# Chunked attention into a token-mixing MLP: k and the two slots of q in three regions, some early clears on ScalarE, a new order of all units

## The chip, the core and the metric

The kernel runs on one core of a Trainium2 chip. The metric is the time of one execution in microseconds of device time. The times before are three runs of the unchanged kernel; the profile is one execution of it.

## The reference

For 8 batches of 8 heads, 576 tokens and a head dimension of 64, attention is computed inside chunks of 64 tokens; its output becomes x, 576 by 512 for each batch. A token mixer then works on x.

```python
scores = scale * np.matmul(q_c, k_c.transpose(0, 1, 2, 4, 3))   # chunks of 64 tokens
attn = np.exp(scores - max); attn = attn / (np.sum(attn, axis=-1, keepdims=True) + 1e-09)
out = np.matmul(attn, v_c)
...
wq = x @ w_q                                  # 512 -> 64
wk = x @ w_k
W_tok = scale * np.einsum('bsd,btd->bst', wq, wk)
mixed = np.einsum('bst,btd->bsd', W_tok, x)
return np.maximum(mixed, 0.0) @ w_out         # 512 -> 512
```

The inputs and the output are float32. The loads cast to float16 on their way.

## The kernel before

**Units.** q and k are cut into 36 units of 1024 rows. A unit is 128 partitions by 512 float16 numbers. All units live in one ring tile, `qk`, with room for 27 units; units 27 to 35 go into the places of units 0 to 8 again. Each unit has three slots: slot 0 holds k, slots 1 and 2 hold q. The rows of q lie in four groups of 32 partitions; groups 0 and 2 go into slot 1, groups 1 and 3 into slot 2, and the other half of each slot must be zero. So there are *clears*: `MZ0_2_1` clears units 0 to 1 of one 32-partition group in the slot that the group's load does not fill (line 145), and `MZ5_9_9` clears both slots of units 5 to 8 at once on 128 partitions (line 142). They are done once; later units land in places whose zeros still stand.

**Loads** (lines 125 to 136) are issued by GpSimd (POOL): `LDk.2_5` brings k of units 2 to 4, `LDq0.2_5` the group 0 of q of the same units, `LDv.12` all of v of batch 1. There are 53 of these loads, the large weight (`LW`) is one more. The loads count on eight semaphores in turn, DMASW0 to DMASW7, so that each issue waits for the landing of the load eight places ahead of it. POOL issues them in order: a load that waits holds up all behind it.

**The chain of one batch.** `TR` (VectorE, DVE, lines 175 and 179) transposes one or two units: first k into a kT tile, then both slots of q into a qT tile. The 20 groups follow the pattern 0-2, 2-4, 4-5, 5-7, 7-9, 9-11, and so on, so that TR0 to TR2 cover units 0 to 4, TR3 and TR4 units 5 to 8, TR5 to TR7 units 9 to 13 (TR7 is unit 13 alone). `SC` (TensorE, PE, line 194) makes the scores of such a group, `EX` (ScalarE, ACT, line 206) the exponentials, `PV` (PE, line 229) the products with v, `RN` (DVE, lines 239 and 240) divides by the sums, three of each for a batch. Then come `XT` (PE transpose), `XE` (its copy), `PJ` and `EP` (projection and copy), `DU`, `WT` and `EW` (a copy and a transpose of the projections), `GM` and `EG` (the product of keys and x), four `MX` with `RL` (mixing and relu) and, 36 in all, `OM` (PE, line 384, the product with w_out) with `OE` (its copy into the ring tile, over units that are no longer needed). `ST` stores three or one of these tiles; all stores wait until the last load of v, `LDv.72`, has landed.

**The order.** Nothing is scheduled by a planner: the string `ORDER` gives the whole program as 430 words, and each engine runs its own words in that order. A letter behind a colon picks the engine of a clear or a copy (D is DVE, A is ACT, P is POOL), a number behind @ picks the PSUM bank. `ZZ4` is four matmuls on a constant tile that nobody reads; they keep TensorE from standing still. `MU` fills that tile, `MO` sets a column of ones in v, `LI` makes identity matrices on POOL, `LS` and `LK` load and cast the small weights. The framework adds semaphore waits between engines: a word that writes a region of a tile waits for the earlier words of `ORDER` that read or wrote it, and one that reads it waits for those that wrote it.

Of the kernel before, what the change touches and what calls it, by code (L numbers as in the profile page):

```python
# [9 lines left out]
F16 = mybir.dt.float16  # L10
F32 = mybir.dt.float32
# [39 lines left out]
def kernel(  # L51
# [10 lines left out]
    nc = tc.nc  # L62
# [3 lines left out]
    P = 128  # L66
# [53 lines left out]
    def load(word):  # L120
# [10 lines left out]
        if it[0] == "k":  # L131
            return nc.gpsimd.dma_start(qk[:, at : at + hi - lo, 0], runs[1][:, lo:hi])
        else:
            i = int(it[1])
            rows = slice(32 * i, 32 * i + 32)
            return nc.gpsimd.dma_start(qk[rows, at : at + hi - lo, 1 + i % 2], runs[0][rows, lo:hi])  # L136
# [388 lines left out]
```

## Time and profile before

| | us |
|---|---|
| median of three runs | 127.6 (126.42 to 129.34) |
| the profiled execution, its own time | 127.21 |
| its span (first to last instruction) | 125.4 |
| PE busy | 95.7 (76%) |
| DVE busy | 92.9 (74%) |
| ACT busy | 67.5 (54%) |
| POOL busy | 49.8 (40%) |

The profiled execution's time is its span and 1.8 us around it. Busy shares are over the whole span; the first matmul starts at 18.05 us and the load queue ends before the stores begin, so the stages have to be looked at one by one. The strips of the profile cut the span into 40 slices of 3.135 us. Sizes of loads in the profile are those in SBUF, in units of 1024 bytes; the rates in its GB/s strip are of bytes written as well.

### The profile page before, as it was taken

To read this page: it belongs to the slowest core of one execution; us is meant where nothing else is said; L and a number is where in the kernel's file an instruction comes from. 1 tells how busy PE (TensorE), PEld (TensorE's weight loads), DVE (VectorE), ACT (ScalarE), POOL (GpSimd) and SP (SyncE) were. 2 spreads that over 40 slices of the span, in tenths; PEclk is the share of its full clock that TensorE was granted. 3 is DMA by queue.
4 is the path that set the end of the run, shared out by engine and by line. 5 is a ranking of instruction groups with operands and counts; after the bars stand their busy time and mean duration, and the time that the engine had idled before them with its cause. 6 is when DMAs were issued, how large, how long until landed. Compare 5 with 4: busy or idle time off the path is not lost.

```text
span 125.4 us, 3815 instructions
## 1 busy us (share of the span) xinstructions
PE 95.7 (76%) x1664; PEld 54.1 (43%) x1664; DVE 92.9 (74%) x136; ACT 67.5 (54%) x111; POOL 49.8 (40%) x64
## 2 busy tenths in 40 slices
PE   0000026788889879988989999999799999999990
PEld 0000024443545555553464555555554756444430
DVE  5402899967687989799899799979698477759220
ACT  0560005212727692498574858989697874544420
POOL 2730799999966139445437684000000000000000
PEclk9999999999999999999999999999999999999999
DMA  2697389999999999999999999999949999119693
GB/s 28 110 186 116 45 67 162 204 180 172 205 202 159 199 200 207 204 184 175 201 188 167 202 205 164 192 182 161 139 83 406 397 417 411 73 63 413 276 368 140
DMA packets 50064, 24.62 MB, mean 196 GB/s; under 512 B 38016, under 2 KB 48256, under 8 KB 50048
## 3 DMA queue, kind: packets, MB, share of 16 engines
q0 software_dynamic: 47456, 14.68, 108.3%
q1 hardware_dynamic: 2592, 9.70, 19.5%
q8 instruction: 13, 0.21, 0.6%
q14 instruction: 3, 0.02, 0.0%
HBM read 29.62 MB, written 9.44 MB: 311 GB/s over the span
## 4 chain that ended last, share of the span: by engine, by line
PE 42%; DMA 19%; POOL 16%; DVE 9%; issue 8%; ACT 4%; DVEq 0%
PE pb L384 21%; DMA wout<-in_moe_w_out_dram 9%; DMA qk<-in_k_dram 7%; POOL qk L136 5%; POOL vt L125 4%; PE pb L250 4%; DMA qk<-in_q_dram 4%; PE pb L276 4%; POOL qk L142 3%; PE pb L348 3%; PE pb L229 3%; PE pb L330 3%; DVE qk L145 2%; PE pb L194 2%; DVE kT L175 2%
## 5 line engine op out<-in xcount | busy, mean ns | idle before, releaser
L384 PE MATMUL pb<-wout,rmx 128*128 128x512 f16 x144 | 35.8, 381 | 0.0
L194 PE MATMUL pb<-qT,kT 64*64 64x128 f16 x576 | 12.9, 229 | 21.1 <-DVE qT L179 20.3
L206 ACT ACTIVATE est<-pb 128x1024 f16<-128x1024 f32 (+1 forms) x20 | 18.5, 941 | 17.7 <-PE pb L194 17.4
L136 POOL DMA_DIRECT2D qk<-in_q_dram x36 | 20.2, 567 | 18.8 <-DMA vt<-in_v_dram 5.9
L240 DVE TENSOR_TENSOR xn<-pb,rec 128x768 f16<-128x768 f32 x24 | 23.0, 957 | 0.8
L175 DVE STREAM_TRANSPOSE kT<-qk 128x512 f32<-128x512 f32 (+1 forms) x20 | 19.9, 997 | 4.4 <-DMA qk<-in_q_dram 3.2
L179 DVE STREAM_TRANSPOSE qT<-qk 128x1024 f32<-128x1024 f32 (+1 forms) x20 | 22.0, 1101 | 0.0
L194 PEld LDWEIGHTS <-kT 64*64 64x64 f16 x576 | 10.4, 113 | 23.5 <-DVE kT L175 17.2
L398 ACT COPY qk<-pb 128x512 f32<-128x512 f32 x26 | 15.1, 591 | 7.8 <-PE pb L384 7.6
L384 PEld LDWEIGHTS <-rmx 128*128 128x128 f16 x144 | 13.2, 104 | 12.3 <-issue 1.2
L125 POOL DMA_DIRECT2D vt<-in_v_dram x8 | 14.7, 1843 | 3.4 <-DMA qk<-in_k_dram 2.4
L266 ACT COPY xT<-pb 128x768 f32<-128x768 f32 (+1 forms) x14 | 9.1, 664 | 11.4 <-PE pb L250 9.6
L364 ACT ACTIVATE rmx<-pb 128x576 f16<-128x576 f32 x20 | 12.6, 653 | 2.7 <-PE pb L348 2.7
L250 PE MATMUL pb<-iden,xn 128*128 128x128 f32 x72 | 11.9, 299 | 0.9 <-DVE xn L240 0.5
L250 PEld LDWEIGHTS pb<-iden,xn 128*128 128x128 f32 x72 | 8.6, 150 | 4.9 <-DVE xn L240 2.4
L396 DVE COPY qk<-pb 128x512 f32<-128x512 f32 x10 | 6.8, 684 | 5.2 <-PE pb L384 5.1
L145 DVE MEMSET qk<- 32x512 f32 (+1 forms) x8 | 4.7, 592 | 7.5 <-DMA qk<-in_q_dram 4.5
L362 DVE TENSOR_SCALAR rmx<-pb 128x576 f16<-128x576 f32 x12 | 8.8, 746 | 1.7 <-PE pb L348 1.6
L417 PE MATMUL pb<-unit 128*128 128x512 f16 x32 | 9.8, 443 | 0.0
L229 PE MATMUL pb<-vt,est 64*64 64x65 f16 x576 | 7.7, 200 | 2.4 <-ACT est L206 2.2
L276 PE MATMUL pb<-xT,wpj 128*128 128x512 f16 (+1 forms) x48 | 9.0, 323 | 0.1
L229 PEld LDWEIGHTS <-est 64*64 64x64 f16 x576 | 6.7, 112 | 5.3 <-issue 3.2
(37 smaller groups left out, 90.7 us busy)
## 6 DMA issues: line engine op xcount, KB each, us to landing
out_dram<-qk SPq DMA_DIRECT2D x11, 768.0 KB, 6.6
vt<-in_v_dram POOLq DMA_DIRECT2D x8, 576.0 KB, 13.2
qk<-in_k_dram POOLq DMA_DIRECT2D x4, 512.0 KB, 12.1
qk<-in_q_dram POOLq DMA_DIRECT2D x16, 128.0 KB, 11.0
qk<-in_k_dram POOLq DMA_DIRECT2D x3, 640.0 KB, 10.3
qk<-in_q_dram POOLq DMA_DIRECT2D x12, 160.0 KB, 9.2
out_dram<-qk SPq DMA_DIRECT2D x3, 256.0 KB, 2.7
wout<-in_moe_w_out_dram POOLq DMA_DIRECT2D x1, 512.0 KB, 11.6
```

Source lines behind the costliest of these rows:

```text
L125: return nc.gpsimd.dma_start(vt[b % NV][:, lo:hi, 0:D], flat[2][b * H * S : (b + 1) * H * S].rearrange("(c p) d -> p c d", p=P)[:, lo:hi],)
L136: return nc.gpsimd.dma_start(qk[rows, at : at + hi - lo, 1 + i % 2], runs[0][rows, lo:hi])
L175: nc.vector.transpose(out=kT[x % NQ][:, 0:n].bitcast(F32).rearrange("p u (x r) o -> p u r (x o)", r=R), in_=src[:, :, 0],)
L179: nc.vector.transpose(out=qT[x % NQ][:, 0:n].bitcast(F32).rearrange("p u m x o -> p u m (x o)"), in_=src[:, :, 1:3].rearrange("p u s r w - ...
L194: nc.tensor.matmul(ps[CH * o : CH * o + CH, bank + f, at : at + P], lhsT=kT[x % NQ][rows, u, CH * j : CH * j + CH, e], rhs=qT[x % NQ][rows ...
L206: nc.scalar.activation(est[x % NE][:, 0 : 8 * n].rearrange("p m (w r) -> p m w r", r=R), src.rearrange("p (m r w) -> p m w r", r=R, w=R), ...
L229: nc.tensor.matmul(ps[CH * o : CH * o + CH, bank + (n + o) % 2, at : at + D + 1], lhsT=est[x % NE][rows, 4 * size * g + 4 * u + 2 * (j // ...
L240: nc.vector.tensor_tensor(out=xn[b % 3][:, 3 * p : 3 * p + 3].rearrange("p t (f i) d -> p i (t f) d", f=2), in0=xv[:, :, :, 0:D], in1=rec[ ...
L250: nc.tensor.transpose(ps[:, bank + at // 4, P * (at % 4) : P * (at % 4) + P], xn[b % 3][:, i].rearrange("p h c -> p (h c)").bitcast(F32), ...
L276: nc.tensor.matmul(to, lhsT=wpl[:, e, :] if part and c else wpj[:, c, e, :], rhs=rhs, start=(c == 0 and e == 0), stop=(c == 1 and e == 1),)
L384: nc.tensor.matmul(ps[:, bank, :], lhsT=c[:, r], rhs=wout[:, i, :], start=(i == 0), stop=(i == NI - 1),)
L398: nc.scalar.copy(os_, ps[:, bank, :])
```

## The change

The ring tile is laid out by slot, not by unit: k of all 27 places, then slot 1 of all, then slot 2 of all. A load of one group of q is then one stretch in each partition, and the two slots of a unit lie 27 units apart. Seven of the eight early clears by group move from DVE to ACT, as an activation with scale 0 of the constant tile, which is now filled first. Of the five large clears, two change from POOL to DVE and two from DVE to POOL. The transposes, the scores and the output tiles use the new layout with the same shapes and counts. The string `ORDER` is new from its first to its last word: every load, clear, transpose, matmul and store may stand at another place. The number of words of each kind is the same, 430 in all. The copies are dealt out anew: 26 of the 32 `RL` go to ACT (20 before), 7 of 8 `DU` (4), 8 of 8 `EG` (6), 3 of 8 `EW` (7).

```diff
-LS MO3 MO1 MZ0_2_1:D MZ2_5_1:D MZ2_5_0:D LDq2.2_5 MO4 LDk.2_5 LDq3.2_5 LDq0.2_5 MZ0_2_0:D LDq1.2_5 MO2 MZ0_2_3:D LK
...
+MU LS MZ2_5_2:A LDq1.0_2 LDk.2_5 LDq2.0_2 LDk.0_2 LDq0.0_2 MO4 MZ0_2_2:A MO3 ZZ4@0 LDq3.0_2 ZZ4@1 LDq2.2_5 MZ0_2_1:A
...
-    qk = sb.tile([P, RING, 3, R * D], F16, name="qk")
+    qk = sb.tile([P, 3, RING, R * D], F16, name="qk")
...
-    qT = [sb.tile([P, 2, 2 * R, 32, 2], F16, name=f"qT{i}") for i in range(NQ)]
+    qT = [sb.tile([P, 2, 2, R, 32, 2], F16, name=f"qT{i}") for i in range(NQ)]
...
-            return nc.gpsimd.dma_start(qk[rows, at : at + hi - lo, 1 + i % 2], runs[0][rows, lo:hi])
+            return nc.gpsimd.dma_start(qk[rows, 1 + i % 2, at : at + hi - lo], runs[0][rows, lo:hi])
...
         if part == 9:
-            e.memset(qk[:, lo:hi, 1:3].bitcast(F32).rearrange("p u s w -> p u (s w)"), 0.0)
-        else:
-            rows = slice(32 * part, 32 * part + 32)
-            e.memset(qk[rows, lo:hi, 2 - part % 2].bitcast(F32), 0.0)
+            e = nc.vector if eng == "D" else nc.gpsimd
+            e.memset(qk[:, 1:3, lo:hi].bitcast(F32).rearrange("p s u w -> p s (u w)"), 0.0)
+            return
+        rows = slice(32 * part, 32 * part + 32)
+        to = qk[rows, 2 - part % 2, lo:hi].bitcast(F32)
+        if eng == "A":
+            nc.scalar.activation(
+                to,
+                unit[rows].bitcast(F32)[:, None].broadcast_to([32, hi - lo, R * D // 2]),
+                AF.Copy,
+                scale=0.0,
+            )
+        else:
+            nc.vector.memset(to.rearrange("p u w -> p (u w)"), 0.0)
...
-        src = qk[:, at : at + n].bitcast(F32).rearrange("p u s (r w) -> p u s r w", w=32)
+        src = qk[:, :, at : at + n].bitcast(F32).rearrange("p s u (r w) -> p s u r w", w=32)
...
-            out=qT[x % NQ][:, 0:n].bitcast(F32).rearrange("p u m x o -> p u m (x o)"),
-            in_=src[:, :, 1:3].rearrange("p u s r w -> p u (s r) w"),
+            out=qT[x % NQ][:, :, 0:n].bitcast(F32).rearrange("p s u r x o -> p s (u r) (x o)"),
+            in_=src[:, 1:3].rearrange("p s u r w -> p s (u r) w"),
...
-                                rhs=qT[x % NQ][rows, u, :, R * j : R * j + R, e],
+                                rhs=qT[x % NQ][rows, :, u, :, R * j : R * j + R, e],
...
-    ob = qk[:].rearrange("p u s w -> p (u s w)").bitcast(F32)
+    ob = qk[:].rearrange("p s u w -> p s (u w)").bitcast(F32)
     OB = (9, 15, 21, 0)
-    UW = 3 * R * D // 2
+    def held(pr, at, size):
+        lo = OB[pr] * R * D // 2 + at % 3 * DM
+        return ob[:, at // 3, lo : lo + size * DM]
```

The instructions move on every engine. Two places matter for what follows. In the rows below, a load on line 136 is one group of q (32 partitions by its number of units by 512), one on line 132 is k, one on line 125 is v, and the names in brackets are the semaphores of other engines or loads that the instruction waits for.

The first loads, POOL's rows before. The first three waits on DVE stand for early clears of the same units (`MZ2_5_0`, `MZ0_2_3`, `MZ0_2_2`).

```order
L136 DMA qk_63<-in_q_dram 32x3x512
L132 DMA qk_63<-in_k_dram 128x3x512 [waits DVE_49]
L136 DMA qk_63<-in_q_dram 32x3x512 x3
L136 DMA qk_63<-in_q_dram 32x2x512 [waits DVE_49]
L132 DMA qk_63<-in_k_dram 128x2x512
L136 DMA qk_63<-in_q_dram 32x2x512 [waits DVE_49]
L136 DMA qk_63<-in_q_dram 32x2x512 [waits DMASW0_49]
L136 DMA qk_63<-in_q_dram 32x2x512 [waits DMASW1_49]
L125 DMA vt0_64<-in_v_dram 128x36x64 [waits DMASW2_49]
```

The same place of the changed kernel, up to the first load of q of units 5 to 8 (`LDq1.5_9`); the row behind it, `LDq3.5_9`, waits for DVE as well:

```order
L136 DMA qk_63<-in_q_dram 32x2x512
L132 DMA qk_63<-in_k_dram 128x3x512
L136 DMA qk_63<-in_q_dram 32x2x512
L132 DMA qk_63<-in_k_dram 128x2x512
L136 DMA qk_63<-in_q_dram 32x2x512 x2
L136 DMA qk_63<-in_q_dram 32x3x512 x2
L136 DMA qk_63<-in_q_dram 32x3x512 [waits DMASW0_49]
L136 DMA qk_63<-in_q_dram 32x3x512 [waits DMASW1_49]
L125 DMA vt0_64<-in_v_dram 128x36x64 [waits DMASW2_49]
L142 MEMSET qk_63 128x2x1024 [waits DMASW7_49,DMASW5_49,DMASW0_49]
L132 DMA qk_63<-in_k_dram 128x4x512 [waits DMASW3_49]
L136 DMA qk_63<-in_q_dram 32x4x512 [waits DMASW4_49,DVE_49,Pool_49]
```

The first loads no longer wait for a clear; the large clear of units 5 to 8, now on POOL behind them, waits for three loads of units 0 to 4, which it does not touch.

The second place is around the transposes of units 9 to 13. DVE's rows before (RN1's last, then TR5, TR6 and TR7):

```order
L240 TENSOR_TENSOR xn1_84<-pb_110,rec0_80 128x2x6x64 [waits DVE_49]
L175 STREAM_TRANSPOSE kT2_71<-qk_63 128x2x8x32 [waits DMASW5_49,DMASW3_49,DMASW6_49,DMASW2_49,DMASW1_49]
L179 STREAM_TRANSPOSE qT2_74<-qk_63 128x1024 [waits Pool_49]
L175 STREAM_TRANSPOSE kT0_69<-qk_63 128x2x8x32
L179 STREAM_TRANSPOSE qT0_72<-qk_63 128x1024
L175 STREAM_TRANSPOSE kT1_70<-qk_63 128x8x32
L179 STREAM_TRANSPOSE qT1_73<-qk_63 128x512
```

DVE's rows of the change at that place (RN1's last, then TR6, TR5 and TR7):

```order
L249 TENSOR_TENSOR xn1_84<-pb_110,rec1_81 128x2x6x64 [waits DVE_49]
L184 STREAM_TRANSPOSE kT0_69<-qk_63 128x2x8x32 [waits DMASW5_49]
L188 STREAM_TRANSPOSE qT0_72<-qk_63 128x1024 [waits DMASW3_49,DMASW4_49,DMASW2_49,DMASW1_49]
L184 STREAM_TRANSPOSE kT2_71<-qk_63 128x2x8x32
L188 STREAM_TRANSPOSE qT2_74<-qk_63 128x1024 [waits DMASW1_49]
L184 STREAM_TRANSPOSE kT1_70<-qk_63 128x8x32
L188 STREAM_TRANSPOSE qT1_73<-qk_63 128x2x256 [waits DMASW3_49,DMASW2_49]
```

And POOL's rows of the change beside them: `LDk.9_14`, `LDv.22`, `LDk.14_18`, `LDq3.14_18`, `LDq0.14_18`, `LDq2.14_18`, `LDq2.18_23`, `LDq1.14_18`:

```order
L132 DMA qk_63<-in_k_dram 128x5x512
L125 DMA vt2_66<-in_v_dram 128x36x64 [waits DMASW6_49]
L132 DMA qk_63<-in_k_dram 128x4x512 [waits DMASW7_49]
L136 DMA qk_63<-in_q_dram 32x4x512 [waits DMASW0_49]
L136 DMA qk_63<-in_q_dram 32x4x512 [waits DMASW1_49,DVE_49]
L136 DMA qk_63<-in_q_dram 32x4x512 [waits DMASW2_49,DVE_49]
L136 DMA qk_63<-in_q_dram 32x5x512 [waits DMASW3_49]
L136 DMA qk_63<-in_q_dram 32x4x512 [waits DMASW4_49]
```

Before, each transpose waits for loads of its own units only. Now the waits go across units: `LDq0.14_18` counts on DMASW1 and waits for TR6, and TR5 waits on DMASW1 for it; `LDq2.14_18` and `LDq2.18_23` count on DMASW2 and DMASW3, the first of them waits for TR5, and TR7 waits for both. The same kind of wait stands at `LDq3.5_9` (for the clear `MZ9_14_9` on DVE, behind TR0 to TR2), at `LDq0.9_14` (for TR4) and at `LDq2.32_36` (for TR16).

61 lines of the change are left out of this document (30 added, 31 removed).

## Prediction

> **What bounds the kernel now.** I read the strips first, then the chain of work that ended last, the stages, and last the rows of DVE and POOL in order of time.
>
> ```profile
> DMA  2697389999999999999999999999949999119693
> GB/s 28 110 186 116 45 67 162 204 180 172 205 202 159 199 200 207 204 184 175 201 188 167 202 205 164 192 182 161 139 83 406 397 417 411 73 63 413 276 368 140
> ```
>
> A slice is 3.135 us. The loads are poor in the first seven slices and then run at about 200 GB/s, never over 207, until the slice that starts at 90 us; the stores follow at up to 417. The stages show when TensorE fills up (time, busy PE, PEld, DVE, ACT, POOL, clock, DMA):
>
> ```profile
> 50.00:66.00 16.00, 14.38 (x261) 8.41 (x262) 14.61 (x21) 11.24 (x20) 7.57 (x12) 1.00 1.62 190
> 66.00:82.00 16.00, 15.51 (x265) 8.40 (x265) 15.11 (x20) 11.98 (x20) 8.27 (x8) 1.00 1.72 187
> 82.00:98.00 16.00, 15.31 (x311) 8.90 (x308) 13.50 (x21) 13.26 (x24) 0.00 (x0) 1.00 1.55 204
> 98.00:114.00 16.00, 16.00 (x243) 8.61 (x241) 10.78 (x19) 9.48 (x15) 0.00 (x0) 1.00 0.69 277
> ```
>
> From 66 to 114 us PE is idle for 48 - 46.82 = 1.2 us. So whatever is late at 66 us is late at the end. The chain says what comes before (start, length, what):
>
> ```profile
> 46.70 8.25 DMA qk<-in_k_dram
> 54.95 1.00 DVE kT L175
> ...
> 60.99 0.42 PE pb L229 x24
> 61.41 0.02 issue
> 61.44 0.24 DVE rec L239
> ...
> 114.40 6.16 PE pb L384 x28
> ```
>
> Behind 61.44 the chain is nearly all PE; ahead of it, a load and DVE's transposes. I therefore follow the change by two milestones on DVE: **the end of TR7** (45.11 us, 44.43 + 0.68) and **the start of RN3** (61.44 us). DVE's rows up to the first:
>
> ```profile
> 9.44 0.70 DVE L145 MEMSET qk<- 32x768 f32 x1 [4.46 <-DMA qk<-in_q_dram]
> 12.44 1.29 DVE L145 MEMSET qk<- 32x512 f32 x2 [2.30 <-DMA qk<-in_k_dram]
> 14.22 1.76 DVE L142 MEMSET qk<- 128x2048 f32 x1 [0.49 <-issue]
> 15.90 1.04 DVE L175 STREAM_TRANSPOSE kT<-qk 128x512 f32<-128x512 f32 x1
> ...
> 20.43 0.67 DVE L179 STREAM_TRANSPOSE qT<-qk 128x512 f32<-128x512 f32 x1
> ...
> 39.84 1.12 DVE L175 STREAM_TRANSPOSE kT<-qk 128x512 f32<-128x512 f32 x1 [0.87 <-DMA qk<-in_q_dram]
> ...
> 44.43 0.68 DVE L179 STREAM_TRANSPOSE qT<-qk 128x512 f32<-128x512 f32 x1
> ```
>
> Clears wait for loads (4.46 and 2.30 us), and POOL waits for clears (5.70):
>
> ```profile
> 1.31 0.70 POOL L136 DMA_DIRECT2D qk<-in_q_dram  x1 [0.86 <-POOLq L509]
> 3.81 0.77 POOL L132 DMA_DIRECT2D qk<-in_k_dram  x1 [1.81 <-DVE qk L145]
> 4.58 2.23 POOL L136 DMA_DIRECT2D qk<-in_q_dram  x4
> 6.80 0.72 POOL L132 DMA_DIRECT2D qk<-in_k_dram  x1
> 13.22 1.58 POOL L136 DMA_DIRECT2D qk<-in_q_dram  x3 [5.70 <-DVE qk L145]
> ```
>
> **The first part: the start.** These waits go. POOL issues its first nine loads in a row: 0.70 for the first, 0.57 for each further one of q, about 0.75 for one of k, so from 1.31 to 6.8 us. DVE's early clears shrink to one; ACT takes seven. The nearest rows:
>
> ```profile
> L398 ACT COPY qk<-pb 128x512 f32<-128x512 f32 x26 | 15.1, 591 | 7.8 <-PE pb L384 7.6
> L240 DVE TENSOR_TENSOR xn<-pb,rec 128x768 f16<-128x768 f32 x24 | 23.0, 957 | 0.8
> L396 DVE COPY qk<-pb 128x512 f32<-128x512 f32 x10 | 6.8, 684 | 5.2 <-PE pb L384 5.1
> L175 DVE STREAM_TRANSPOSE kT<-qk 128x512 f32<-128x512 f32 x16 | 17.5, 1092 | 4.4 <-DMA qk<-in_q_dram 3.2 <-PE pb L194 1.1
> L179 DVE STREAM_TRANSPOSE qT<-qk 128x1024 f32<-128x1024 f32 x16 | 19.3, 1208 | 0.0
> ```
>
> A copy of 512 numbers takes ACT 0.59 us; three clears of 768 (0.59 x 768/512 = 0.88) and four of 512 make 5.0 us beside ACT's first casts, done by about 10 us. ACT then waits for the first scores, which come at 18.05 now: cost nothing, 1 us at most if they run at half that pace. But DVE now has two large clears ahead of TR0, and the first waits for `LDq3.2_5`, `LDq3.0_2` and `LDq1.2_5`. Behind the first load those nine bring 1120 KB = 1.15 MB. In the profile k and q of units 2 to 4 (480 KB) took 4.57 us behind their issue, 2.6 of it at 186 GB/s, so 1.9 are latency: 2.8 + 1.9 + 1.15 MB at 186 GB/s (6.2) = 10.9. By the pace of before (992 KB landed 8.5 us after the first k issue, at 12.3) it is 11.6. I take 11.0. The clears cost 2.2 (1.76 x 2560/2048) and 1.76 us: **TR0 starts at 15.0, where the first transpose starts at 15.90 now.** A gain of 0.9, not the 6 us that the waits promise.
>
> **The second part: round trips.** TR0 to TR2 take 5.2 us (15.90 to 21.10), to 20.2; `MZ9_14_9`, now on DVE, 2.2 more, to 22.4. `LDq3.5_9` waits for it on POOL, and with it the identities and the other loads of units 5 to 8:
>
> ```profile
> 20.20 0.25 POOL masks.py:197 MEMSET iden<- 128x128 f32 x1
> ...
> 20.88 0.28 POOL L169 CAST ident<-iden 128x128 f16<-128x128 f32 x1
> 21.12 1.08 POOL L136 DMA_DIRECT2D qk<-in_q_dram  x2
> ```
>
> 0.57 + 0.96 + 1.08 bring POOL to 25.0. What a landing costs is in the issues (KB each, median us to landing):
>
> ```profile
> vt<-in_v_dram POOLq DMA_DIRECT2D x8, 576.0 KB, 13.2
> qk<-in_q_dram POOLq DMA_DIRECT2D x16, 128.0 KB, 11.0
> qk<-in_q_dram POOLq DMA_DIRECT2D x4, 64.0 KB, 2.4
> ```
>
> 2.4 us on a near-empty queue, 11.0 on a full one. Here it is near empty: 27.4. RN0, three times a reciprocal and 0.96 us of line 240, 3.4 in all, covers the wait up to 25.8. TR3 ends at 28.6, TR4 at 30.7. Only then may `LDq0.9_14` go, and with it all of units 9 to 13, 1280 KB: 2.4 for the first 64 KB and 1.25 MB at 200 GB/s, 6.2, so k lands at 39.3. RN1 is over at about 36.5 by then, so DVE waits. TR6 ends at 41.4. Now `LDq0.14_18` is released; its own road is 0.57 + 2.4, to 44.4, but `LDv.22`, `LDk.14_18` and `LDq3.14_18`, issued just behind k, are ahead of it in the queue: 576 + 512 + 128 + 128 = 1344 KB, 6.9 us from 39.3, so it lands at 46.2. TR5's qT (1.2) ends at 47.4. That releases `LDq2.14_18`, with `LDq2.18_23` behind it: 1.1 + 2.4, to 50.9; TR7's qT 0.7, **to 51.6 us against 45.11: 6.5 late.** Bounds: at 2.4 us for every landing behind k and the earlier end (10.4) at the start it is 49.2, 4.1 late; with full-queue landings (11.0) it would be over 60, which needs loads that POOL cannot issue while it is blocked.
>
> **The third part: less on DVE.** Behind TR7 one group of scores (0.4), one exponential (0.6, as a copy of 512) and PV2 (0.42 in the chain) take 1.6 us with their hand-overs, RN2 3.4. Up to RN3 DVE then has TR8, RL1.1, TR9, three copies, TR10 and TR12: 3 x 2.1 + 0.75 (a relu, a little over a copy) + 3 x 0.68 + 1.2 = 10.3, so RN3 starts at 66.9, **5.5 late**; 1.0 is won back because the copies went to ACT, which is busy 11.24 of 16 us in that stage and has room.
>
> **The fourth part: v of batch 5.** `LDv.52` stands behind `LDq2.32_36`, which waits for TR16. Today's stretch from PV4 to PV5 in the chain:
>
> ```profile
> 72.52 0.57 PE pb L229 x47
> ...
> 82.31 0.31 PE pb L229 x23
> ```
>
> 9.2 us, 73.09 to 82.31. In the new order it has one OM more (6.16/7 = 0.88) and GM4 and XT4.0 less (about 0.8 and 0.4), 8.9 us, before PE needs that v. RN4.2, TR14 and TR16 take 1.2 + 2.1 + 2.1, and the two loads 2.4 + 640 KB at 200 GB/s (3.3): 11.1. PE stands for 2.2; I take **2.0**, with 0 and 3 as ends. Nothing hides it, since PE is full there.
>
> Other edits cost nothing that the rows can show: stores and output copies have the same sizes, and a scores matmul reads the same 128 columns in one more dimension; if that cost 10%, 12.9 us of line 194 would give 1.3, unlikely as the steps between columns stay the same.
>
> **The sum**, against the profiled execution's own 127.21 (the median of the three runs, 127.6, lies 0.4 above): + 5.5 + 2.0 = 134.7 us. It stays behind the last store as now.
>
> **Rivals.**
>
> Faster loads, the other side. If the queue moved 400 GB/s where it is not full, as it does for stores, TR0 would start at 11.6 (7.6 + 4.0), k of units 9 to 13 land at 32.8, TR6 end at 34.9, `LDq0.14_18` land at 37.9 by its own road and TR7 end at 43.3: 1.8 early, 1.0 more to RN3, no stall for v: 124.4. It decides from about 350 GB/s. Against it: no slice of loads shows over 207, in the third slice not over 186.
>
> No round trip at all: the waits are all met when they are reached. Then DVE goes on without a gap: TR4 at 30.0, RN1 to 35.5, TR7 at 40.9; 4.2 + 1.0 early, 122.0. For it: the waits sit behind 10 to 20 us of other work in the order. Against it: TR5 waits for a load that TR6 releases, with 0 us of DVE work between.
>
> Cheap round trips: TR7 at 49.2, 4.1 - 1.0 late and no stall for v, 130.3. A little more luck is within 2%.
>
> A cold TensorE. The same scores group and the same idle matmuls, early and later:
>
> ```profile
> 18.05 1.07 PE L194 MATMUL pb<-qT,kT 64*64 64x128 f16 x32 [18.05 <-DVE qT L179]
> 28.66 1.91 PE L417 MATMUL pb<-unit 128*128 128x512 f16 x4
> 31.14 0.65 PE L194 MATMUL pb<-qT,kT 64*64 64x128 f16 x32 [0.57 <-DVE qT L179]
> ```
>
> After a long pause a group takes 1.65 times as long, and this lasts for some 12 us of broken work, though the clock strip shows 9 throughout. The new order lets PE stand for 3 us and more at TR6, TR5 and TR7, and I put its 12 early idle matmuls (5 to 6 us from 1.5 on) down as lost, since SC0 starts at 17. If PE goes cold at TR7, its 7 us of work up to RN3 take 4.5 more, half of it on the path: 137.0.
>
> The Trainium skill, "TensorE: Matmul & The Clock Gate", section "Part 1: The HAM clock gate", has that as a rule: the array runs at half rate until about 3.4 us of sustained work, and again after an idle window of that length. The 1.07 and 0.65 us agree in kind; no gap of over 3.4 us behind 31 us is in this trace to show the way back. By that rule the time would be near the 137.0.
>
> **How the numbers follow.** Forecast 134.7: 0.50. Cold TensorE 137.0: 0.14. Cheap round trips 130.3: 0.18, of which 0.08 within 2% of 127.2 (124.7 to 129.8; 2% is about what a measurement of this kernel can tell from no change). Faster loads 124.4: 0.11, half of it, 0.06, within 2%. No round trip 122.0: 0.07. So slower 0.50 + 0.14 + 0.10 = 0.74, same 0.14, faster 0.12. The range leaves out the faster cases and the far end of the cold one: 126.5 to 138.5. The forecast's own range is 130 to 138.
>
> **What would show it.** TR0's start near 15 us, with a clear ahead of it that waits for a load of q; POOL waiting for DVE's line 142 clear, then for DVE's qT transposes (line 188), several us each; DVE's qT transposes waiting for loads of q, two of them for 3 us or more, and TR7's end near 51; a weight load of line 238 (PV) waiting for v between 85 and 95 us. I am wrong if the load strip is full from slice 3 to 12, if the round trips are under 3 us each, or if the PE stage from 66 us on turns out to have had slack, so that RN3 is late and the end is not.

## The result, and the profile after

| | before | changed |
|---|---|---|
| median, same chip | 127.13 us (4 runs) | 155.33 us (4 runs) |
| the profiled execution | 127.21 | 155.73 |
| its span | 125.4 | 154.0 |

The ratio of the times is 1.221, with a 95% interval of 1.207 to 1.235. Some executions of one kernel are a few per cent longer than its others: medians are of all runs, ratios of the shorter ones, and the profiles of `split_both`, `split_mz`, `mv14`, `warm` and `split_both_fewv` are of longer ones. The forecast was 134.7 us, with a range up to 138.5: the sign was right, the size was not. The loss is 28 us, not 7.5.

The strips of the changed kernel (a slice is 3.85 us; TensorE's busy tenths, its granted clock, DMA's busy tenths, GB/s):

```profile
PE   6500068777508127999999995380969869999970
...
PEclk9965555699995955799999999655599999999997
DMA  3999911799999379999599596099999499039795
GB/s 47 165 190 140 167 28 14 100 146 126 166 158 192 60 112 168 195 167 190 86 115 112 86 151 108 2 81 173 193 159 133 188 408 411 24 128 416 299 388 204
```

The load strip has holes in its whole length: 28 and 14 GB/s from 19 to 27 us, 60 in the slice that starts at 50, a sag from 73 us on and 2 GB/s in the slice that starts at 96 us. Before, the loads had no such hole from 22 us to their end. TensorE has pauses now between 38 and 58 us and again between 92 and 108 us. Who waited for whom (us in total, times, longest):

```profile
POOL qk L136 <- DVE qT L188: 45.8, 7, 11.3
...
PE pb L203 <- DVE qT L188: 32.1, 8, 12.9
...
DVE qT L188 <- DMA qk<-in_q_dram: 11.8, 5, 4.4
...
DVE kT L184 <- DMA qk<-in_k_dram: 9.5, 2, 5.3
DVE qk L142 <- DMA qk<-in_q_dram: 9.5, 1, 9.5
...
POOL qk L136 <- DVE rec L248: 7.1, 1, 7.1
```

The kinds of wait are the ones that the prediction named: POOL stands for DVE's transposes of q (line 188), 45.8 us in all, and DVE for loads of q and k. POOL's rows (start, length, what, idle time before it and what ended it) show where:

```profile
25.04 0.55 POOL L136 DMA_DIRECT2D qk<-in_q_dram  x1 [7.08 <-DVE rec L248]
...
33.71 2.30 POOL L136 DMA_DIRECT2D qk<-in_q_dram  x4 [2.50 <-DVE qT L188]
47.01 0.55 POOL L136 DMA_DIRECT2D qk<-in_q_dram  x1 [6.99 <-DVE qT L188]
53.69 1.66 POOL L136 DMA_DIRECT2D qk<-in_q_dram  x3 [6.14 <-DVE qT L188]
...
75.63 1.08 POOL L136 DMA_DIRECT2D qk<-in_q_dram  x2 [11.28 <-DVE qT L188]
84.92 0.59 POOL L136 DMA_DIRECT2D qk<-in_q_dram  x1 [6.39 <-DVE qT L188]
98.81 0.56 POOL L136 DMA_DIRECT2D qk<-in_q_dram  x1 [10.50 <-DVE qT L188]
99.73 1.84 POOL L125 DMA_DIRECT2D vt<-in_v_dram  x1 [0.37 <-PE pb L203]
...
105.96 3.64 POOL L125 DMA_DIRECT2D vt<-in_v_dram  x2
```

The first row is `LDq3.5_9`, which waited for the clear `MZ9_14_9` (it ends at 24.74; the division that the row names stands behind the load in `ORDER`, so it cannot be the cause); then come `LDq0.9_14` behind TR4, `LDq0.14_18` behind TR6 and `LDq2.14_18` behind TR5. These were all in the prediction. The rows at 75.63, 84.92 and 98.81 are `LDq0.23_27` behind TR12, `LDq3.27_32` behind TR13 and `LDq2.32_36` behind TR16, 28 us of standing in all; of them the prediction had only the last, with its v of batch 5. The last two loads of v, at 105.96, went out 33 us earlier before the change:

```profile
73.11 3.62 POOL L125 DMA_DIRECT2D vt<-in_v_dram  x2 [0.35 <-PE pb L229]
```

The Trainium skill, "DMA: Bandwidth & Descriptors", section "Anatomy of one DMA — SWDGE (gpsimd) path", says that a DMA engine waits for no semaphore; the wait is on the engine that issues. The trace agrees: the wait of 10.50 us up to 98.81 stands in POOL's row, and the queue behind it runs dry, from 151 and 108 GB/s to 2 in the slice that starts at 96 us.

DVE's rows, the two milestones and the second place:

```profile
12.50 2.19 DVE L142 MEMSET qk<- 128x2560 f32 x1 [9.46 <-DMA qk<-in_q_dram]
...
16.80 1.12 DVE L184 STREAM_TRANSPOSE kT<-qk 128x512 f32<-128x512 f32 x1
...
44.56 1.09 DVE L184 STREAM_TRANSPOSE kT<-qk 128x512 f32<-128x512 f32 x1 [5.33 <-DMA qk<-in_k_dram]
...
52.15 1.25 DVE L188 STREAM_TRANSPOSE qT<-qk 128x1024 f32<-128x1024 f32 x1 [4.45 <-DMA qk<-in_q_dram]
...
57.67 0.71 DVE L188 STREAM_TRANSPOSE qT<-qk 128x512 f32<-128x512 f32 x1 [3.74 <-DMA qk<-in_q_dram]
...
76.97 0.23 DVE L248 RECIPROCAL rec<-pb 128x12 f32<-128x12 f32 x1 [0.20 <-PE pb L238]
...
85.58 0.23 DVE L248 RECIPROCAL rec<-pb 128x12 f32<-128x12 f32 x1
...
95.58 1.09 DVE L184 STREAM_TRANSPOSE kT<-qk 128x512 f32<-128x512 f32 x1 [4.14 <-DMA qk<-in_k_dram]
...
108.11 0.23 DVE L248 RECIPROCAL rec<-pb 128x12 f32<-128x12 f32 x1 [4.26 <-PE pb L238]
```

TR7 ends at 58.4 us (45.1 before), RN3 starts at 76.97 (61.44) and RN4 at 85.58. Batch 5's first division, RN5, starts at 108.11. The last two were, before:

```profile
71.59 0.22 DVE L239 RECIPROCAL rec<-pb 128x12 f32<-128x12 f32 x1
...
82.75 0.23 DVE L239 RECIPROCAL rec<-pb 128x12 f32<-128x12 f32 x1 [0.65 <-PE pb L229]
```

RN5 hangs in the chain on v of batch 5:

```profile
99.73 7.67 DMA vt<-in_v_dram
107.44 0.55 PE pb L238 x21
```

Five points of DVE's rows divide the loss. "To the end" is the span less RN5's start:

| us | TR0 | TR7's end | RN3 | RN4 | RN5 | RN4 to RN5 | RN5 to the end |
|---|---|---|---|---|---|---|---|
| before | 15.90 | 45.11 | 61.44 | 71.59 | 82.75 | 11.2 | 42.7 |
| changed | 16.80 | 58.38 | 76.97 | 85.58 | 108.11 | 22.5 | 45.9 |

So of the 28.6 us of span, RN3 has 15.5; 1.5 are won back up to RN4, RN4 to RN5 loses 11.4, and the last stretch 3.2.

### The profile page after: what moved, and what is told of

Its sections match the earlier page's. It is cut to its first block, busy times and chain, and to the rows that moved or that the text cites. A ratio compares the mean times of both kernels' runs of the same rounds, so it can differ in the third digit from the quotient of the medians.

```text
span 154.0 us, 3822 instructions
## 1 busy us (share of the span) xinstructions
PE 104.7 (68%) x1664; PEld 58.7 (38%) x1664; DVE 88.1 (57%) x123; ACT 77.6 (50%) x125; POOL 47.1 (31%) x63
## 4 chain that ended last, share of the span: by engine, by line
PE 37%; DMA 23%; issue 16%; DVE 12%; POOL 8%; ACT 1%; DVEq 0%; POOLq 0%
PE pb L397 16%; DMA qk<-in_q_dram 14%; DVE qT L188 5%; DMA vt<-in_v_dram 5%; POOL qk L136 4%; DMA qk<-in_k_dram 4%; PE pb L339 4%; PE pb L203 4%; PE pb L259 3%; PE pb L285 3%; PE pb L238 3%; PE pb L357 3%; DVE qk L142 2%; DVE kT L184 2%; POOL qk L132 2%
## 5 line engine op out<-in xcount | busy, mean ns | idle before, releaser
L136 POOL DMA_DIRECT2D qk<-in_q_dram x36 | 20.2, 565 | 60.6 <-DVE qT L188 45.8
L203 PE MATMUL pb<-qT,kT 64*64 64x128 f16 x576 | 15.2, 253 | 32.1 <-DVE qT L188 32.1
L397 PE MATMUL pb<-wout,rmx 128*128 128x512 f16 x144 | 36.6, 395 | 0.0
L203 PEld LDWEIGHTS <-kT 64*64 64x64 f16 x576 | 12.0, 128 | 35.1 <-DVE qT L188 14.3
L373 ACT ACTIVATE rmx<-pb 128x576 f16<-128x576 f32 x26 | 16.2, 655 | 3.7 <-PE pb L357 3.6
L238 PE MATMUL pb<-vt,est 64*64 64x65 f16 x576 | 9.5, 211 | 7.1 <-DMA vt<-in_v_dram 4.3
L430 PE MATMUL pb<-unit 128*128 128x512 f16 x32 | 12.1, 542 | 1.5 <-DVE unit L446 1.5
L248 DVE RECIPROCAL rec<-pb 128x12 f32<-128x12 f32 x24 | 5.4, 225 | 12.0 <-PE pb L238 9.5
L142 DVE MEMSET qk<- 128x2560 f32 (+1 forms) x3 | 6.1, 2050 | 10.3 <-DMA qk<-in_q_dram 9.5
L238 PEld LDWEIGHTS <-est 64*64 64x64 f16 x576 | 8.2, 121 | 9.7 <-DMA vt<-in_v_dram 5.8
L285 PE MATMUL pb<-xT,wpj 128*128 128x512 f16 (+1 forms) x48 | 9.8, 345 | 0.1
```

Source lines behind the costliest of these rows:

```text
L136: return nc.gpsimd.dma_start(qk[rows, 1 + i % 2, at : at + hi - lo], runs[0][rows, lo:hi])
L203: nc.tensor.matmul(ps[CH * o : CH * o + CH, bank + f, at : at + P], lhsT=kT[x % NQ][rows, u, CH * j : CH * j + CH, e], rhs=qT[x % NQ][rows ...
L238: nc.tensor.matmul(ps[CH * o : CH * o + CH, bank + (n + o) % 2, at : at + D + 1], lhsT=est[x % NE][rows, 4 * size * g + 4 * u + 2 * (j // ...
L285: nc.tensor.matmul(to, lhsT=wpl[:, e, :] if part and c else wpj[:, c, e, :], rhs=rhs, start=(c == 0 and e == 0), stop=(c == 1 and e == 1),)
L373: nc.scalar.activation(dst, src, AF.Relu, scale=scale_moe)
L397: nc.tensor.matmul(ps[:, bank, :], lhsT=c[:, r], rhs=wout[:, i, :], start=(i == 0), stop=(i == NI - 1),)
```

## The experiments

**Theory.** A transposition of q, or a large clear, is one instruction over both slots of its units. In the new layout the two slots lie 27 units apart, and the semaphores are laid as if the instruction touched what lies between them as well. So loads of later units wait for transpositions and clears of earlier ones, and the other way round; POOL issues in order and stands. **Rivals:** the new order is bad in itself; far regions are slow to read; the loss is TensorE's clock; only the clears matter.

**Two halves of the change, and the two wide instructions.** Four kernels on one chip, before 127.69 us there. `split_both` is the changed kernel with this edit, for the clears and the transpositions:

```diff
-            e.memset(qk[:, 1:3, lo:hi].bitcast(F32).rearrange("p s u w -> p s (u w)"), 0.0)
+            for s in (1, 2):
+                e.memset(qk[:, s, lo:hi].bitcast(F32).rearrange("p u w -> p (u w)"), 0.0)
...
-        nc.vector.transpose(
-            out=qT[x % NQ][:, :, 0:n].bitcast(F32).rearrange("p s u r x o -> p s (u r) (x o)"),
-            in_=src[:, 1:3].rearrange("p s u r w -> p s (u r) w"),
-        )
+        for s in range(2):
+            nc.vector.transpose(
+                out=qT[x % NQ][:, s, 0:n].bitcast(F32).rearrange("p u r x o -> p (u r) (x o)"),
+                in_=src[:, 1 + s].rearrange("p u r w -> p (u r) w"),
+            )
```

> The changed kernel (new layout, new order) with each large clear and each transposition of q made in two instructions, one per slot of q, so that no instruction reaches over both regions. Theory (waits between units: an instruction that covers both slots also counts as touching what lies between them in memory, so loads of later units wait for transposes and clears of earlier ones, and the reverse): the waits of POOL for line 188 and of DVE for loads of q go, TR7 ends before 45 us and RN5 starts before 83; the time falls from 155 to 119 to 127 us, although DVE has some 19 instructions more (about 1 to 2 us of its time). Rival 'the new order is bad': stays at 145 to 156. Rival 'reading q out of two far regions is slow in itself': stays above 145, or the pieces take longer in sum by far more than 1 us. Rival 'cold TensorE': the waits go, but the time stays above 140, since the early pauses are the order's own.

128.54 us, ratio to before 0.998 (0.990 to 1.005): nearly the whole loss is gone by this edit alone, though the median stays a little above the 119 to 127 of the theory. `order_old_layout` is the other half of the change:

```diff
-    qk = sb.tile([P, 3, RING, R * D], F16, name="qk")
+    qk = sb.tile([P, RING, 3, R * D], F16, name="qk")
...
```

> The layout of before (k and both slots of q side by side per unit) with the new order and the clears on ScalarE. Theory (waits between units come from the new layout): only waits within a unit remain, 120 to 129 us, with early waits of POOL for clears as before. Rival 'the new order is bad': 145 to 156 us, with the same late TR7 (over 55 us). Rival 'far regions are slow in themselves': 120 to 129, as the theory.

136.19 us, ratio 1.068 (1.059 to 1.077). This is neither the theory's 120 to 129 nor the rival's 145 and more. POOL waits for no transposition here, but DVE's first clear waits for a load of its own units:

```profile
15.77 0.70 DVE L153 MEMSET qk<- 32x768 f32 x1 [13.90 <-DMA qk<-in_q_dram]
```

TR0 starts at 21.5, RN5 at 86.7, 4.0 us later than before, and behind RN5 it takes 47.7 us, 5.0 more than before. `layout_old_order` has the new layout and this edit:

```diff
-MU LS MZ2_5_2:A LDq1.0_2 LDk.2_5 LDq2.0_2 LDk.0_2 LDq0.0_2 MO4 MZ0_2_2:A MO3 ZZ4@0 LDq3.0_2 ZZ4@1 LDq2.2_5 MZ0_2_1:A
+LS MO3 MO1 MZ0_2_1:D MZ2_5_1:D MZ2_5_0:D LDq2.2_5 MO4 LDk.2_5 LDq3.2_5 LDq0.2_5 MZ0_2_0:D LDq1.2_5 MO2 MZ0_2_3:D LK
...
```

> The new layout with the order of before. Theory (waits between units): the same kind of waits at the places that this order gives them, POOL waiting for line 188 several times, 135 to 160 us. Rival 'the new order is bad': within 3% of before, 124 to 131. Rival 'far regions are slow in themselves': 130 to 160 without long waits of POOL for line 188.

157.66 us, ratio 1.235 (1.219 to 1.250): the loss does not need the new order. One row tells the four apart, POOL's loads of q (busy time and mean; idle time before them, and what ended it). The changed kernel, the old order in the new layout, the new order in the old layout, both splits:

```profile
L136 POOL DMA_DIRECT2D qk<-in_q_dram x36 | 20.2, 565 | 60.6 <-DVE qT L188 45.8 <-DVE rec L248 7.1 <-issue 3.2
```

```profile
L136 POOL DMA_DIRECT2D qk<-in_q_dram x36 | 20.3, 569 | 57.6 <-DVE qT L188 44.9 <-DVE qk L142 6.6 <-DVE rec L248 3.4
```

```profile
L136 POOL DMA_DIRECT2D qk<-in_q_dram x36 | 20.2, 569 | 24.3 <-DMA vt<-in_v_dram 8.4 <-ACT qk L143 5.6 <-DVE rec L247 4.3
```

```profile
L136 POOL DMA_DIRECT2D qk<-in_q_dram x36 | 20.1, 564 | 17.1 <-DMA vt<-in_v_dram 8.2 <-DMA qk<-in_k_dram 4.0 <-DVE wkn L326 1.6
```

The waits for line 188 are there where a transposition reaches over both regions, whatever the order, and in no other kernel. With both splits POOL waits for landings, that is, for a full queue, and the strip of loads shows no hole up to 88 us (slices of 3.17 us):

```profile
GB/s 41 150 206 143 163 207 177 171 202 194 166 201 203 206 204 182 174 205 172 182 207 190 166 200 175 159 125 118 409 399 323 8 0 0 124 413 310 372 373 153
```

Far regions are not slow to read. The 16 large transpositions of q in the changed kernel:

```profile
L188 DVE STREAM_TRANSPOSE qT<-qk 128x1024 f32<-128x1024 f32 x16 | 19.5, 1220 | 8.1 <-DMA qk<-in_q_dram 8.1
```

That is 1220 ns each, and 1208 before. That the semaphores count what lies between is inferred from where the waits are; that they come from these instructions is shown. All of POOL's seven waits for line 188 in the changed kernel fit it. Six are for groups 0 and 2, whose slot 1 is the first of the two, and their places in the ring lie above those of the transposition (`LDq0.23_27` behind TR12, unit 22); the seventh is for group 3, in slot 2, with places below (`LDq3.27_32`, places 0 to 4, behind TR13, units 23 and 24). `LDq3.14_18`, in slot 2 with places above, had no such wait.

`split_tr` has the second half of that diff alone.

> The changed kernel with only the transpositions of q made in two, one per slot; the large clears still reach over both regions. Theory: POOL's waits for line 188 and DVE's for loads of q at TR5, TR7, TR15 and TR16 go; what is left are the clears' waits (a clear that waits for a load of q up to about 12 us, and POOL that waits some 7 us for the clear of units 9 to 13): TR0 near 16.8 as now, 124 to 137 us. Rival 'the clears are the cause': above 145. Rival 'the new order is bad': above 145.

139.26 us, ratio 1.090 (1.077 to 1.104), above the 124 to 137 of the theory, but no rival's 145. Line 188's waits are gone, and the clears keep TR0 at 16.9; splitting the clears as well is worth 10.7 us more. `split_mz` has the first half alone (before 126.37 us on its chip):

> The changed kernel with only the large clears made in two, one per slot; the transpositions of q still reach over both regions. Theory (waits between units): POOL's waits for line 188 stay at some 40 us in all, the clear that waited 9.5 us for a load of q starts early, and TR0 with it, by 3 us or more; what it gains is the 155 to 129 us of both splits less the 155 to 139 of the other one, so 145 us, between 142 and 151. Rival 'the clears are the cause': 126 to 135. Rival 'cold TensorE': under 3 us of gain, since the later pauses stay.

151.24 us, but the two runs are 154.69 and 147.78, so its size is open between 1 and 8 us. The profiled one (154.69) has TR0 at 10.1, RN3 at 72.2 and RN5 at 103.4, which is 6.7, 4.7 and 4.7 us earlier, and POOL still waits 50.7 us in all for the transpositions. The clears are a part of the loss; that they are the smaller one rests on `split_tr`, which wins 16.1 us with the clears left wide.

**Which of the two places costs what.** `split_tr_first` splits the transpositions TR0 to TR9 only, `split_tr_last` TR10 to TR19 only (before 128.08 us):

```diff
+        for s in range(2) if x < 10 else ():
+            nc.vector.transpose(
...
+        if x < 10:
+            return
         nc.vector.transpose(
...
```

> The changed kernel with the transpositions of q made in two only for TR0 to TR9; those from TR10 on and the large clears still reach over both regions. Theory: POOL's waits of 2.5, 7.0 and 6.1 us for TR4, TR6 and TR5 go, RN3 starts near 67, the later three waits (11, 6 and 10 us) stay; 145 to 151 us. If the later waits grow by what the first ones shrink (POOL just arrives earlier at them): 151 to 156.

143.62 us: 11.7 less than the changed kernel, more than the 4 to 10 that the 145 to 151 of the theory allow. RN3 starts at 64.8 (76.97), RN4 to RN5 still takes 21.4 us, and POOL's later waits are 8.3, 6.3 and 9.2 us.

> The changed kernel with the transpositions of q made in two only for TR10 to TR19. Theory: RN3 starts near 77 as in the changed kernel; the stretch from RN4 to RN5 shrinks from 22.5 us to 11 to 15, and the time falls by 8 to 11 us, to 144 to 148. If the second place cost only the 2.0 us that the prediction gave it: 152 to 154.

150.00 us: 5.3 less. RN4 to RN5 takes 13.1 us, so 9.4 of the 11.4 us go there, as the theory had it; the time gained falls short of its 8 to 11, since RN3 was 1.6 us later in this execution and the last stretch 1.7 us longer. The two places nearly add up: 11.7 + 5.3 = 17.0, and both together (`split_tr`) give 16.1. (These kernels ran on several chips, with medians before of 126.37 to 128.08 us, so differences between them are good to about 1 or 2 us.)

**The wait, or what is queued behind it.** `mv14` moves three loads in `ORDER` (before 126.37 us here and in the two kernels behind it):

```diff
-TR6 MX0.3@4 SC6@0 PJ1@2 RL0.2:A LDq0.14_18 TR5 LDq2.14_18 SC5@6 EX6 EP1:A LDq2.18_23 TR7 EX5
+TR6 MX0.3@4 SC6@0 PJ1@2 RL0.2:A TR5 SC5@6 EX6 EP1:A TR7 LDq0.14_18 LDq2.14_18 LDq2.18_23 EX5
```

> The changed kernel with three loads of q (of units 14 to 22) moved in the order behind TR7, so that TR6, TR5 and TR7 no longer wait for loads that are released by one another. Theory: the two round trips at TR5 and TR7 (4.45 and 3.74 us of DVE's waiting) go, TR7 ends near 51 where it ends at 58.4 us now, and the time falls by 4 to 8 us, to 147 to 151. Rival 'the loads are the bound whatever the transposes do' (the queue is empty just as long, since POOL waits for TR7 instead): TR7 ends early, but the time falls by less than 3 us, to 152 to 156.

152.34 us (151.18 and 153.49): the median is in the rival's range, the shorter run just outside it and at the upper end of the theory's, so the time does not decide between them. The rows of the profiled run (153.49) tell more. DVE's, TR5's q, TR7's q, and TR8:

```profile
47.67 1.20 DVE L188 STREAM_TRANSPOSE qT<-qk 128x1024 f32<-128x1024 f32 x1
...
49.23 0.67 DVE L188 STREAM_TRANSPOSE qT<-qk 128x512 f32<-128x512 f32 x1
...
57.96 1.11 DVE L184 STREAM_TRANSPOSE kT<-qk 128x512 f32<-128x512 f32 x1
62.98 1.25 DVE L188 STREAM_TRANSPOSE qT<-qk 128x1024 f32<-128x1024 f32 x1 [3.91 <-DMA qk<-in_q_dram]
```

TR7 ends at 49.9, 8.5 us earlier, and RN3 starts at 76.13, 0.8 earlier. Both round trips are gone from DVE, but POOL now stands 10.1 us in one piece, for TR7, and TR8 waits for the loads that go out behind it. `mv2nd` leaves the waits for transpositions and moves only loads that have no such wait:

```diff
-TR12 MX2.1@6 LDq0.23_27
+TR12 MX2.1@6 LDv.42 LDk.27_32 LDq0.23_27
...
-EX13 LDq3.27_32
+EX13 LDv.52 LDk.32_36 LDq3.27_32
```

> The changed kernel with v of batch 4 and k of units 27 to 31 moved ahead of the load that waits for TR12, and v of batch 5 and k of units 32 to 35 ahead of the load that waits for TR13; nothing else is moved, the waits themselves stay. Theory (POOL's waits cost because of the loads queued behind the waiting one): TR16's wait for k (4.1 us), the wait for v of batch 5 (4.3 us of idle TensorE at 107 us) and the cold stretch in front of it go, and the time falls by 6 to 12 us, to 143 to 149. Rival 'the transposes' own waits for q cost it': under 3 us, 152 to 156.

149.54 us, ratio 1.183 (1.164 to 1.202), 5.8 less than the changed kernel's 155.33 and 4.8 by the ratios: just short of the theory's 6 to 12, and nearer to it than to the rival's under 3. RN4 to RN5 takes 13.4 us in place of 22.5 (RN4 is 3.7 later), although POOL still stands for 39.4 us in all for line 188. So a good part of the price of these waits is what stands behind them in POOL's queue.

**The clock.** `warm` adds idle matmuls in the pauses:

```diff
-SC0@0
+ZZ4@0 ZZ4@0 ZZ4@0 ZZ4@0 ZZ4@0 ZZ4@0 ZZ4@0 ZZ4@0 ZZ4@0 ZZ4@0 ZZ4@0 SC0@0
...
-SC16@6
+ZZ4@6 ZZ4@6 ZZ4@6 SC16@6
...
```

> The changed kernel with idle matmuls added on TensorE in its pauses: 44 of 128x512 ahead of the first scores, 16 and 12 and 12 ahead of the scores that wait for TR6, TR5 and TR7, 12 each ahead of the scores of TR16 and ahead of PV5. Theory (the waits are the cause, the clock is an addition): the group of 32 scores matmuls goes from 1.07 to 0.65 us at the three late places and the eight output matmuls behind 99 us from 3.6 to about 1.9, in sum 2 to 5 us off the path, so 150 to 154. Rival 'cold TensorE is the main loss': 8 us or more, under 147. If the clock needs nothing of it: 155.

155.47 us (154.22 and 156.72; the changed kernel's four runs lie between 154.14 and 157.96), nothing gained where 2 to 5 us were expected. The granted clock was 0.89 from 44 to 60 us and 1.00 from 98 to 107.4 (0.68 and 0.50 in the changed kernel). TensorE's rows:

```profile
47.84 0.65 PE L204 MATMUL pb<-qT,kT 64*64 64x128 f16 x32 [1.68 <-DVE qT L189]
...
99.02 0.65 PE L204 MATMUL pb<-qT,kT 64*64 64x128 f16 x32 [0.29 <-DVE qT L189]
99.60 1.91 PE L398 MATMUL pb<-wout,rmx 128*128 128x512 f16 x8
...
108.45 0.55 PE L239 MATMUL pb<-vt,est 64*64 64x65 f16 x24 [4.35 <-DMA vt<-in_v_dram]
```

The scores take 0.65 us (1.07 in the changed kernel at the same places), the eight output matmuls 1.91 (3.60), and PV5 starts at 108.45 where it starts at 107.44 without the idle matmuls. The cold stretches are real, and up to PV5 they lie in time that is spent waiting for loads.

**What bounds the kernel without the waits.** Two kernels leave out the loads of v of batches 3 to 7, `split_both_fewv` and `before_fewv` (before 127.19 us):

```diff
             b, f = int(rng[0]), int(rng[1])
+            if b > 2:
+                return last["v.22"]
...
-                            rhs=vt[b % NV][rows, n // 2, 0 : D + 1],
+                            rhs=vt[b % 3][rows, n // 2, 0 : D + 1],
```

> split_both without the loads of v of batches 3 to 7 (these batches read the v of batches 0 to 2 again, so the output is another one): 2.88 MB less in the load queue, 14.4 us at the 200 GB/s that it moves. Theory 'with the waits gone the new order stands against the load queue' (DMA is at 9 tenths up to 88 us in split_both, and its last PV at 92 us waits for the last v): the last PV comes 8 us or more earlier and the time falls to 112 to 121. Rival 'TensorE is the bound, as the prediction put it for before': 125 to 130.

124.95 us (123.93 and 125.97), 3.6 less than `split_both`, and the last PV 3 us earlier: the load queue is a part of its bound, not the 8 us and more that I expected, and the time lies beside the rival's 125 to 130.

> The kernel before without the same loads of v. The prediction's reading (PE is idle for 1.2 us from 66 to 114 us, so the loads there are no bound): 124 to 128, last PV near 101 as now. Rival 'the load queue bounds this kernel too': 112 to 121.

125.71 us, ratio 0.991 (0.987 to 0.995). The loads are no bound of the kernel before, as the prediction read it: 14 us less of loading are worth 1.1 us by the ratio.

**The new layout in the old order, without the wide instructions.** `old_order_split` is `layout_old_order` with both splits, `old_order_split_act` has seven of its early clears on ScalarE too (`MZ2_5_1:D` becomes `MZ2_5_1:A`, and so on). Before 128.08 us:

> The new layout with the order of before, and each large clear and each transposition of q made in two, one per slot. Theory (the loss is the waits between units; the layout itself takes away the early waits between loads and clears of one unit): the wait of POOL for a clear (5.7 us in before) and DVE's for loads before its clears are gone, the first transposition starts 2 to 6 us earlier than the 15.9 us of before, TensorE is as dense behind it, and 20 more instructions on DVE cost about 1 us: 121 to 126 us. Rival 'the start is hidden' (TensorE and the loads set the end anyway): 126 to 129. Rival 'far regions are slow in themselves': over 129.

122.62 us, ratio 0.956 (0.949 to 0.963): **faster than both kernels.** DVE's first transposition, 15.90 us before:

```profile
9.42 1.04 DVE L185 STREAM_TRANSPOSE kT<-qk 128x512 f32<-128x512 f32 x1
```

> The same, with seven of the eight early clears of 32 partitions on ScalarE in place of DVE. If DVE's clears set the start: 1 to 3 us earlier than the kernel with the clears on DVE, 119 to 125. If the loads set it: the same within 1 us.

122.92 us, ratio 0.959 (0.954 to 0.965), the same: the loads set the start.

Beside `split_both`, which starts as early (TR0 at 9.56), this shows the share of the order and of the copies that it deals out anew: 0.998 against 0.956, some 5 us. RN5 starts at 76.5 there and at 77.7 here, but behind it the new order needs 50.2 us and the old one 42.8. The stage in which they part (busy PE, PEld, DVE, ACT, POOL, clock, DMA, GB/s), new order, then old:

```profile
82.00:98.00 16.00, 12.19 (x267) 7.01 (x268) 8.97 (x16) 8.65 (x14) 0.00 (x0) 0.88 1.08 276
```

```profile
82.00:98.00 16.00, 15.26 (x342) 8.92 (x341) 12.06 (x21) 12.55 (x23) 0.00 (x0) 1.00 1.22 276
```

TensorE stands for 3.8 of 16 us in the new order and for 0.7 in the old one. (`split_both`'s profiled execution took 128.51 us; its ten runs lie between 126.21 and 131.94.) `cand1` tried to fill the longest of these pauses with one output block:

```diff
-GM5@5 OE19:A XT6.0@4
+GM5@5 OE19:A OM20@4 OE20:A XT6.0@4
```

> split_both with output block 20 (four matmuls, 0.86 us, and its copy on ScalarE) moved from behind XT7.1 to ahead of XT6.0, into the pause of 3.3 us in which TensorE waits for RN6 on DVE. If TensorE is the bound of the last 30 us: 0.9 us earlier, and the pause is shorter than the ones behind which the granted clock fell, so 125.0 to 127.5 in the median, not over 128.5. If the end hangs on the loads alone or the moved copy delays XE6: 127.5 to 129.5.

131.15 us, ratio 1.018 (1.011 to 1.026), where `split_both` has 0.998: no gain but a loss. XT6 now waits for the moved copy, and runs at half clock:

```profile
97.61 2.18 PE L261 MATMUL pb<-iden,xn 128*128 128x128 f32 x9 [0.68 <-ACT qk L413]
```

The stretch behind RN5 takes 50.2 us as in `split_both`, where a part of these transposes runs at half clock too (0.50 from 97.6 to 100.9 us), so the rows do not show where the loss arises. What in the new order's last stretch costs the rest stays open.

## Why the prediction was wrong in its size

**The mechanism** was right: loads that wait for transpositions, a POOL that stands, and a sign that followed from it. The runs with one or both wide instructions split show it as the cause.

**The first part** (a start at 15.0) was off by 1.8: the clear ahead of TR0 ran at 12.50, behind a load of q, not at 11.0, and TR0 started at 16.8. "The 6 us that the waits promise" were there all the same, as `old_order_split` and `split_mz` show with TR0 at 9.42 and 10.1; it was the large clears over both regions that held them back.

**The second part**, 6.5 us at TR7, measured 13.3. Each step was late by a little more than the one before: `LDq3.5_9` was issued at 25.0 (22.4 in the prediction), `LDq0.9_14` at 33.7 (30.7), k of units 9 to 13 was taken up at 44.6 (39.3), TR5's q at 52.2 (46.2), TR7 ended at 58.4 (51.6). The largest single step is k's landing: 10.9 us behind the first issue of its group, where 8.6 were reckoned at 200 GB/s. Up to about 34 us the queue still moved v of batch 1, at 158 GB/s, which the sum did not have in the way; then it moved 89 and 87 GB/s up to 36 us and 154 in the mean from 37 to 43.

**The third part** failed in kind: "1.0 is won back" to RN3. It lost 2.2 (15.5 late at RN3, 13.3 at TR7), and `mv14` shows why. The sum counted DVE's work from TR7 to RN3 as if its loads were there; but every load behind the round trips is late too. In that run an 8.5 us earlier TR7 gave RN3 0.8.

**The fourth part** is the step that failed most: 2.0 us for v of batch 5, bounds 0 to 3. The stretch lost 11.4. The sum followed one load behind one wait. There were three waits, for TR12, TR13 and TR16, with k of units 27 to 31 behind the second, 28 us of a standing POOL in all: the prediction had not looked for loads of later units behind the other transpositions. `split_tr_last` takes 9.4 of the 11.4 away, and `mv2nd`, which only moves v and k ahead of two of these waits, 9.1 (with RN4 3.7 us later).

**What the prediction did not have at all**: the end of the new order. Behind RN5 it loses 3.2 us here, and 7.5 in `split_both` against before (50.2 and 42.7); the comparison of the two orders stopped at PV5. "So whatever is late at 66 us is late at the end" held for before (`before_fewv`: 1.1 us for 14 us of loads), but in the changed kernel it is a lower bound, since the loads run out a second time.

**The rivals.** A cold TensorE (137.0): the cold stretches came, but keeping TensorE busier changed nothing (155.47). The Trainium skill's rule, "TensorE: Matmul & The Clock Gate", section "Part 1: The HAM clock gate", that an idle window of about 3.4 us halves the clock, agrees with two of TensorE's rows of `mv2nd`:

```profile
46.89 1.07 PE L203 MATMUL pb<-qT,kT 64*64 64x128 f16 x32 [5.88 <-DVE qT L188]
...
86.94 0.65 PE L203 MATMUL pb<-qT,kT 64*64 64x128 f16 x32 [3.06 <-DVE qT L188]
```

But the length of one pause does not settle it. In `split_both` four output matmuls went from 1.04 to 1.67 us, with a clock of 0.50 from 84.0 to 87.2 us, and the longest pause ahead of them was 2.39 us; TensorE was busy for 1.41 us of the 3.8 from 80 to 83.8:

```profile
78.32 1.04 PE L399 MATMUL pb<-wout,rmx 128*128 128x512 f16 x4
...
82.53 0.55 PE L261 MATMUL pb<-iden,xn 128*128 128x128 f32 x3 [2.39 <-issue]
...
83.62 1.67 PE L399 MATMUL pb<-wout,rmx 128*128 128x512 f16 x4
```

By the rule the time would have been near 137.0; up to PV5, its price is nothing that `warm` could show. Faster loads: no slice of loads shows over 207 GB/s in `split_both` either. No round trip at all (122.0): `split_both` has none, and TR7's end at 38.1; it takes 128.5: RN5 starts 6.3 us earlier than before, and the new order's end takes 7.5 longer.

## What to carry to other kernels

When a layout moves two things apart that one instruction handles together, look at each such instruction as if it touched all that lies between, and ask which loads of later work now wait for it; two narrower instructions cost little beside one such wait (about 1 us of DVE's time for 20 more transpositions of q here, against 16 us). Much of the price of a wait on an engine that issues loads is the work that stands behind it in its queue, so follow every load behind each wait up to the last one, not only to the first milestone. And compare two orders to the end of the program: an order that reaches each milestone earlier can still end later.

## What the runs showed of the hardware that was not expected

Loads of v move more slowly than loads of q and k. Where the trace has only packets of 128 bytes, which are v's, the rate is 158 GB/s in every kernel looked at (40 to 41 us before, 22 to 24 of `split_both`, 32 to 33.7 of the changed kernel); where it has only packets of 1024 bytes, those of q and k, a full queue moves 202 to 205 (32 to 36 us before, 28 to 30 of `split_both`). The dips of `split_both`'s strip to 171, 166 and 174 GB/s are v. Behind an empty queue the rate was uneven: in the changed kernel it came to 204 GB/s from 36 to 37 us, but was 154 in the mean from 37 to 43, with q and k alone, and 206 from 48 to 50. Why it fell in between is open.

And a clock that fell to half (0.59 in the mean from 98 to 114 us of the changed kernel) cost no time that `warm` could show. From 98.56 to 107.44 us the chain holds 1.10 us of scores and then 7.67 us of waiting for v, so little of the slow work stands in it. Behind 107.44 the chain is TensorE's, at half clock up to 111 us; `warm` ran at half clock there too, so the part of the last stretch's 3.2 us that this costs is not shown. The two stages (columns as above):

```profile
82.00:98.00 16.00, 12.39 (x256) 7.15 (x254) 10.35 (x14) 12.41 (x21) 3.16 (x5) 0.99 0.78 99
98.00:114.00 16.00, 10.12 (x180) 5.70 (x180) 9.14 (x13) 6.00 (x9) 8.41 (x8) 0.59 1.44 132
```
